# Holding DMA transposes behind the weight loads, and loading states and first x in longer rows, in a one-core attention and MLP kernel

## The chip, the cores and the metric

The kernel runs on one core of a Trainium2 chip. The metric is the device time of one execution in microseconds (us). Its profile is one profiled execution of the same program; times in it are counted from the first instruction.

Engine names: PE is the matrix engine (TensorE), DVE the vector engine, ACT the scalar engine, POOL GpSimd, SP the sync engine. POOL and SP issue transfers here as well: POOL through a software queue (it builds the descriptors itself, and can change the type on the way), SP and ACT through hardware queues.

## What is computed

For 8 batches of 8 heads, with x of 512 rows and state of 32 rows, each 64 wide, x attends to state and state attends to x; the 544 rows that come out per batch then pass through an MLP of 512 -> 2048 -> 512 with a squared ReLU, a factor s and a summand b.

```python
def _attn_ref(x, state):                      # x (8, 8, 512, 64), state (8, 8, 32, 64)
    scores = scale * np.matmul(x, state.transpose(0, 1, 3, 2))
...
    xread = np.matmul(softmax(scores), state)
    scores2 = scale * np.matmul(state, x.transpose(0, 1, 3, 2))
...
    sread = np.matmul(softmax(scores2), x)
    return np.concatenate([xread, sread], axis=2)

def _moe_ref(x, w_in, w_out, s, b):           # x (8 * 544, 512)
    r = np.maximum(x @ w_in, 0.0)
    return (s * (r * r) + b) @ w_out
```

All inputs and the output are float32; inside, the kernel works with float16 operands.

## The kernel before

**Stages of a batch.** x is laid out with 128 rows on the partitions (tile `xn`) and transposed to `xT`; for batches 0 and 1 by 16 PE matmuls with an identity (`att_xT_pe`), for batches 2 to 7 by four DMA transposes that SP issues (`att_xT_dma`, L568). States are doubled (`st16`) and transposed into `stT` (`att_st`). `part_T` makes the scores T = state x xT in 16 small matmuls, each using a part of the PE array ("tiled" mode). ACT takes their exponential E with the row sums (L663). A matmul with a block matrix of ones (`bones16`) gives the column sums D, ACT makes their reciprocal by Ln and Exp, DVE multiplies: the normalized weights `a4` (L710). `part_M` multiplies state by a quarter of the input weights (`wi`), which gives M; so x's read and the first MLP layer are one product of a4 and M (`layer1`, 8 groups of four matmuls a batch; ACT does the ReLU at L808, DVE the square at L818). The state's side: E is transposed by two DMA transposes that SP issues (`att_turn`, L730, tile `aT`), `part_V` multiplies it with xn (32 small matmuls, "V"), and the result of all batches waits until the end (`layer1_slots`). The second layer is plain for batch 0 (`layer2_first`, 64 matmuls with `wo`) and, for the others, a scheme of seven products in place of eight (`layer2`) on sums that DVE makes of the activations (`pair_sums`) and of the weights (`weight_sums`, L937).

**What orders the work.** A planner written in the kernel (`Plan`) records every operation with the engines that may do it, an estimated duration, what it reads and writes and a priority. `Plan.order` then goes through a modelled time and hands out the next operation to the engine where it can start first; the order found is issued engine by engine and never changes on the chip. Every engine runs its list in order: an instruction that waits holds all that stands behind it on that engine. A transfer has a duration `lag`: negative for loads that queue behind each other (`MB = 3.05`), positive for others. What the planner believes is only an order; on the chip an instruction waits for the data that it reads, and for the earlier users of the tile that it writes, and for nothing else. `att_turn` names `wo[3]`, the last weight load, in its `rd` list, so that the planner places the transposes behind it; but the transposes do not read `wo[3]`.

**The loads.** SP loads x of batch 0 in four pieces as float32 into `u` (L356: 128 partitions x 2 heads, rows of 256 elements = 1 KB), and ACT casts each to `xn` (L339). ACT issues the identity, the ones matrix (`bones`) and two pairs of states (`stf`). POOL issues, as software transfers with a cast, in this order: wi 0, wi 1, wo 0, x of batch 1, wi 2, wo 1, wi 3, wo 2, s, b, wo 3, the states of batches 2 to 7 (L417, tile `st`), x of batch 2. At most eight software transfers are under way: the ninth is issued when the first has landed, and so on. Later x loads are each issued behind a `gate` copy (L438) that reads the end of the previous batch's xT. POOL also issues the stores of the results (L989).

**Start.** DVE clears `warm` and PE runs 13 matmuls on it (128x512) ahead of its first real one, and a few in later gaps, chosen by the planner.

**Buffers.** PSUM is used as three pairs of banks (`ps`, in the profile "pair") and two single banks (`o`). SBUF has, among others, five `xn`, nine `g`, eight `pd`, four `u`, two `aT` and two `xT` tiles.

Of the kernel before, what the change touches and what calls it, by code (L numbers as in the profile page):

```python
# [14 lines left out]
class Op:  # L15
    def __init__(self, n, engs, fn, rd, wr, prio, mode, lag, gap):
        self.n, self.engs, self.fn, self.prio, self.mode = n, engs, fn, prio, mode
        self.lag, self.gap = lag, gap
        self.units = []
        for key in (*rd, *wr):  # L20
            if key[0] not in self.units:
                self.units.append(key[0])
        self.before = set()
        self.start = self.seen = None


class Plan:
# [10 lines left out]
    LAT = {"PE": 0.24, "ACT": 0.16, "DVE": 0.15, "POOL": 0.15}  # L38
# [23 lines left out]
    def op(self, engs, fn, rd=(), wr=(), prio=5, mode=None, lag=0.0, gap=0.0, into=(), lands=None):  # L62

        o = Op(len(self.ops), engs, fn, rd, [*wr, *((u,) for u in into)], prio, mode, lag, gap)
# [17 lines left out]
    def order(self, warm):  # L82
        free = dict.fromkeys(("PE", "ACT", "DVE", "POOL", "SP"), 0.0)
        free.update(PE=1.2, ACT=2.4, DVE=1.3, POOL=0.5, SP=0.6)
        load_free = 6.0
# [12 lines left out]
        def earliest(o, e):  # L98
            t = max(free[e], o.gap)
            for p in o.before:  # L100
                if p.eng == e and e == "PE":
                    s = p.start
                elif p.eng == e and e in ("SP", "POOL") and p.lag == 0.0:
# [21 lines left out]
        while ready:  # L125
# [39 lines left out]
            if o.lands:  # L165
                o.seen = o.lands
            elif o.lag < 0:

                begin = max(load_free, t + dur + 1.2)
                load_free = begin - o.lag  # L170
                o.seen = load_free + 0.9
            elif o.lag:
                o.seen = max(t + dur, min(load_free, t + dur + 15)) + o.lag
            else:
                o.seen = t + dur + self.LAT[e]
# [19 lines left out]
    SLACK = 0.1  # L195
# [8 lines left out]
def kernel(  # L204
# [18 lines left out]
    P = 128  # L223
# [44 lines left out]
    def PR(kind, b):  # L268
# [22 lines left out]
    st16 = sb("st16", [B * NG, 2, D])  # L291
# [12 lines left out]
    wsum = sb("wsum", [DM], FP32)  # L304
# [3 lines left out]
    bones_dr = nc.inline_tensor(  # L308
        np.kron(np.eye(4), np.ones((Ns, Ns))).astype(np.float16), name="bones_const"
    )  # L310
    st_v = state.rearrange("b (g hf) j d -> (hf j) (b g) d", g=NG)

# [3 lines left out]
    nc.vector.memset(thirty2, 1.0 / Ns)  # L316

# [7 lines left out]
    nc.scalar.dma_start(bones16, bones_dr.ap())  # L325
# [16 lines left out]
    MB = 3.05  # L342

    xf_u = [plan.unit(("u", i), "u") for i in range(2)]
    x0_v = x[0].rearrange("h (q c) d -> q h (c d)", q=P)
    xn = [plan.unit(("xn", b), "xn") for b in range(B)]

    def xf_ap(i):
        return plan.slots["u"][i // 2].bitcast(FP32).rearrange(
            "p (h f) -> p h f", h=4  # L350
        )[:, 2 * (i % 2) : 2 * (i % 2) + 2]

    def x0_load(i):
        op(
            {"SP": 0.5},
            lambda e: nc.sync.dma_start(xf_ap(i), x0_v[:, 2 * i : 2 * i + 2]),  # L356
            wr=[K(("xf", i))],
            prio=0,
            lands=(3.9, 4.7, 6.2, 6.7)[i],
        )  # L360

    def x0_cast(i):
        op(
            {"ACT": 0.55, "DVE": 0.45},
            lambda e: copy(
                e,
                T(xn[0])[:, 2 * i : 2 * i + 2].rearrange("p h c d -> p h (c d)"),
                xf_ap(i),
            ),
            rd=[K(("xf", i))],  # L370
            wr=[K(xn[0], i)],
# [3 lines left out]
    def x_load(b, h0, n, prio, rd=()):  # L375
# [9 lines left out]
            lag=-MB * n / H,  # L385
        )

    def wi_load(c, prio):
# [9 lines left out]
            lag=-MB,  # L398
        )

    def wo_load(q, prio):
# [9 lines left out]
            lag=-MB,  # L411
        )

    def st_load(prio):
        op(
            {"POOL": 1.2},
            lambda e: nc.gpsimd.dma_start(out=st16[:, 2 * NG :, 0], in_=st_v[:, 2 * NG :, :]),  # L417
            rd=[g0],
            wr=[K(("st", 2, 0))],
            prio=prio,  # L420
            lag=-1.6,
        )

    def small_load(dst, src, name, prio):
# [6 lines left out]
            lag=-0.05,  # L431
# [14 lines left out]
    for i in range(4):  # L446
# [14 lines left out]
        lambda p: st_load(p),  # L461
        lambda p: x_load(2, 0, H, p),
    ]
# [4 lines left out]
    def att_st(b0, n, tag, prio, rd=()):  # L468
        u = plan.unit(("stps", b0), tag)

        def view():
            t = T(u) if tag == "o" else T(u).rearrange("p a f -> p (a f)")
            return t.bitcast(FP16).rearrange("p (n q) -> p n q", q=P)
# [11 lines left out]
        if b0 < 2:  # L485
            op(
                {"DVE": 0.25},
                lambda e: nc.vector.tensor_copy(
                    st16[:, b0 * NG : b0 * NG + n], stf[b0].unsqueeze(2).to_broadcast((P, n, 2, D))
                ),  # L490
                wr=[key],
                prio=prio,
                gap=(4.9, 7.5)[b0],
            )
        else:
            op(
                {"DVE": 0.08 + 0.02 * n},
                lambda e: nc.vector.tensor_copy(
                    st16[:, b0 * NG : b0 * NG + n, 1], st16[:, b0 * NG : b0 * NG + n, 0]
                ),  # L500
                rd=[K(("st", 2, 0)), *rd],
                wr=[key],
                prio=prio,
            )
        op({"PE": 0.056 * n}, tr, rd=[key], wr=[K(u)], prio=prio, mode="full")
        op(
            {"DVE": 0.1 + 0.07 * n},
# [3 lines left out]
            prio=prio,  # L511
        )
# [16 lines left out]
    def att_xT_pe(b):  # L529
        u = [plan.unit(("xTps", b, i), "ps") for i in range(2)]  # L530

        def view(i):
            return T(u[i])[:, 0].bitcast(FP16).rearrange("p (h k q) -> p h k q", h=4, k=2)

        for i in range(2):

            def tr(e, i=i):
                for hh in range(4):
                    for k in range(2):
                        mm(  # L540
                            view(i)[:, hh, k, :],
                            T(xn[b])[:, 4 * i + hh, 2 * k : 2 * k + 2, :].rearrange("p c d -> p (c d)"),
                            ident16,
# [700 lines left out]
```

## Time and profile before

| | |
|---|---|
| three runs | 214.95, 215.41, 218.27 us; median 215.41 |
| profiled execution | span 211.4 us from first to last instruction; its own time outside the span is not listed |
| PE | 201.0 us busy (95%), 1966 matmuls |
| DVE, ACT, POOL | 163.8 us (77%), 111.3 us (53%), 42.1 us (20%) |
| software queue | 15360 packets, 15.40 MB |
| SP's hardware queue | 25792 packets, 8.13 MB |

The page gives busy time by engine and by line, the waits by what ended them, and the chain of work that ended last. L242 is the line of the matmul helper, so matmuls are told apart by the tiles that they write and read. A line "DMA xn<-in_x_dram" in the chain is the time from the issue of a load to its landing.

### The profile page before, as it was taken

What the parts mean: (1) busy time and instruction counts of PE and PEld (TensorE: products, weight loads), DVE (VectorE), ACT (ScalarE), POOL (GpSimd) and SP (SyncE); (2) the same over time, 40 slices, a digit from 0 to 9 for tenths busy, and PEclk for the clock granted to TensorE, in tenths of its full rate; (3) what the DMA queues carried; (4) which work ended last, traced back from release to release, by engine and by line L of the source; (5) the groups of instructions that cost most, each with busy time, mean ns of one, the idle gap of its engine ahead of it and who ended that gap; (6) DMA issues with size and microseconds to landing.
All of it is one profiled execution on the core that took longest, in us unless ns stands there. A gap on an engine that the chain in (4) does not pass through costs nothing.

```text
span 211.4 us, 4751 instructions
## 1 busy us (share of the span) xinstructions
PE 201.0 (95%) x1966; PEld 132.3 (63%) x1966; DVE 163.8 (77%) x309; ACT 111.3 (53%) x154; POOL 42.1 (20%) x64
## 2 busy tenths in 40 slices
PE   7985699999999999999999999999999999999992
PEld 2432343445746764767575755776588588888882
DVE  0664779999579989997995989976996697675452
ACT  3594599700778779563877588714910780040000
POOL 5820300042131140303411141114111111111000
PEclk9999999999999999999999999999999999999999
DMA  6999999558798596496596741222011210112132
GB/s 188 220 190 157 207 198 168 93 157 112 166 138 119 102 119 205 76 158 134 72 202 127 82 131 53 50 65 99 12 51 56 85 50 30 57 68 97 55 124 74
DMA packets 42007, 24.04 MB, mean 114 GB/s; under 512 B 26369, under 2 KB 40193, under 8 KB 41985
## 3 DMA queue, kind: packets, MB, share of 16 engines
q0 software_dynamic: 15360, 15.40, 39.6%
q1 hardware_dynamic: 25792, 8.13, 21.0%
q8 instruction: 15, 0.25, 0.5%
q10 hardware_dynamic: 832, 0.20, 0.4%
q14 instruction: 8, 0.06, 0.1%
HBM read 17.37 MB, written 8.91 MB: 124 GB/s over the span
## 4 chain that ended last, share of the span: by engine, by line
PE 81%; DMA 8%; DVE 5%; ACT 2%; POOL 1%; issue 1%
PE o L242 47%; PE pair L242 34%; DMA xn<-in_x_dram 7%; ACT E L663 2%; DVE g L818 1%; DVE u L937 1%; DMA ident<-ident_const 1%; POOL wi L391 1%; DVE xT L339 1%; DVE M L339 1%; POOL wo L404 0%; DVE osb L1026 0%; DVE bias_bc L980 0%; ACT a L703 0%; DVE wsp L966 0%
## 5 line engine op out<-in xcount | busy, mean ns | idle before, releaser
L808 ACT ACTIVATE g<-pair 128x1024 f16<-128x1024 f32 x64 | 61.2, 1035 | 26.6 <-PE pair L242 26.6
L242 PE MATMUL pair<-a,M 128*128 128x512 f16 x256 | 59.6, 379 | 0.2
L242 PEld LDWEIGHTS <-g 128*128 128x128 f16 x424 | 40.9, 98 | 18.3 <-issue 3.0
L242 PEld LDWEIGHTS <-pd 128*128 128x128 f16 x480 | 46.3, 98 | 8.9 <-issue 2.5
L818 DVE TENSOR_TENSOR g<-g 128x1024 f16<-128x1024 f16 x64 | 43.1, 685 | 9.0 <-ACT g L808 9.0
L242 PE MATMUL o<-wo,g 128*128 128x256 f16 (+1 forms) x304 | 44.9, 295 | 0.2 <-DVE osb L1026 0.2
L242 PE MATMUL o<-u,pd 128*128 128x256 f16 x360 | 42.5, 273 | 0.0
L242 PEld LDWEIGHTS <-M 128*128 128x128 f16 x256 | 25.0, 98 | 26.4 <-issue 0.4
L989 POOL DMA_DIRECT2D out_dram<-osb x28 | 18.7, 671 | 95.3 <-DVE osb L1097 38.0
L1085 DVE SCALAR_TENSOR_TENSOR osb<-o,s_bc,bias_bc 128x512 f32<-128x512 f32 (+1 forms) x32 | 22.8, 714 | 10.5 <-PE o L242 10.1
L1097 DVE SCALAR_TENSOR_TENSOR osb<-o,s_bc,osb 128x512 f32<-128x512 f32 (+1 forms) x24 | 17.2, 715 | 8.9 <-PE o L242 8.7
L663 ACT ACTIVATE E<-pair 128x512 f16<-128x512 f32 x16 | 9.4, 593 | 25.9 <-PE pair L242 25.9
L899 DVE TENSOR_TENSOR pd<-g 128x1024 f16<-128x1024 f16 (+1 forms) x32 | 20.7, 653 | 0.2
L339 DVE CAST M<-pair 128x1024 f16<-128x1024 f32 x16 | 19.5, 1218 | 1.7 <-PE pair L242 1.6
L339 ACT CAST M<-pair 128x1024 f16<-128x1024 f32 x16 | 16.1, 1014 | 7.9 <-PE pair L242 7.9
L242 PE MATMUL o<-u,g 128*128 128x256 f16 x120 | 16.7, 273 | 0.0
L242 PE MATMUL o<-wo,pd 128*128 128x256 f16 x120 | 14.6, 273 | 0.0
L907 DVE TENSOR_TENSOR pd<-g,pd 128x512 f16<-128x512 f16 (+1 forms) x32 | 12.6, 403 | 0.2
L910 DVE TENSOR_TENSOR pd<-g,pd 128x512 f16<-128x512 f16 (+1 forms) x32 | 12.6, 403 | 0.2
L858 ACT ACTIVATE g<-pair 128x256 f16<-128x256 f32 x16 | 5.3, 381 | 12.7 <-PE pair L242 12.7
L766 POOL COPY srd<-srdT 128x128 f16<-128x128 f16 x8 | 7.6, 950 | 19.6 <-DMA srdT<-sr 19.6
L242 PE MATMUL pair<-wi,stT 64*32 64x512 f16 x256 | 10.3, 382 | 0.5 <-DMA wi<-in_moe_w_in_dram 0.5
(52 smaller groups left out, 125.0 us busy)
## 6 DMA issues: line engine op xcount, KB each, us to landing
out_dram<-osb POOLq DMA_DIRECT2D x28, 256.0 KB, 2.7
xn<-in_x_dram POOLq DMA_DIRECT2D x7, 512.0 KB, 6.8
wi<-in_moe_w_in_dram POOLq DMA_DIRECT2D x4, 512.0 KB, 12.8
wo<-in_moe_w_out_dram POOLq DMA_DIRECT2D x4, 512.0 KB, 19.1
u<-in_x_dram SPq DMA_DIRECT2D x4, 256.0 KB, 4.3
out_dram<-osb SPq DMA_DIRECT2D x4, 256.0 KB, 2.5
out_dram<-osb SPq DMA_DIRECT2D x4, 128.0 KB, 2.3
xT<-xn SPq DMA_TRANSPOSE x24, 2.5
```

Source lines behind the costliest of these rows:

```text
L242: return nc.tensor.matmul(out, lhsT, rhs, start=start, stop=stop, tile_position=tp, is_transpose=is_transpose, skip_group_check=True,)
L339: (nc.scalar.copy if e == "ACT" else nc.vector.tensor_copy)(dst, src)
L663: nc.scalar.activation(T(E[b])[:, g, :].rearrange("p (m t) -> p m t", m=2), T(u)[:, :, hS * g : hS * g + hS], AF.Exp, scale=scale, accum_o ...
L766: lambda e: nc.gpsimd.tensor_copy(srd[:, :, :, b], srdT[:, b]),
L808: lambda e, u=u, j=j, p=p: nc.scalar.activation(g_view(G[b, j])[:, 2 * p : 2 * p + 2], T(u), AF.Relu),
L818: nc.vector.tensor_mul(t, t, t)
L899: nc.vector.tensor_tensor(view()[:, :, 0:2], blocks(b, j)[:, :, 1:2, :].to_broadcast((P, 2, 2, n)), blocks(b, j)[:, :, 0:4:3, :], ALU.subt ...
L907: nc.vector.tensor_tensor(view()[:, :, 2], blocks(b, j)[:, :, 3], view()[:, :, 0], ALU.subtract)
L910: nc.vector.tensor_tensor(view()[:, :, 3], blocks(b, j)[:, :, 2], view()[:, :, 2], ALU.subtract)
L989: lambda e: eng(e).dma_start(dst, src()),
L1085: lambda e: nc.vector.scalar_tensor_tensor(t_view(u), o_view(bank), s_bc, bias(h), ALU.mult, ALU.add),
L1097: lambda e: nc.vector.scalar_tensor_tensor(t_view(u), o_view(bank), s_bc, t_view(u), ALU.mult, ALU.add),
```

## The change

1. **Transposes of E for batches 0 and 1.** `att_turn(b, True)` now has POOL copy two elements of `wo[3]` into each half of `aT` (the new helper `after`). The transpose writes the same tile, so it waits for the copy, and the copy waits for the last weights.
2. **States of batches 2 to 7.** The software load with cast, the DVE copy that doubles them, the 12 PE transposes (128x128) and the DVE copy go. In their place: after a like copy of two elements, SP loads 96 rows of 1024 float32 (4 KB) into a `pd` buffer; two POOL copies (96x1024, float32 to float16) double them into another `pd` buffer; 16 PE transposes (96 columns) go into one PSUM pair; ACT or DVE copies the pair to `stT`.
3. **x of batch 0.** Pieces are cut so that a partition holds eight rows (512 elements, 2 KB) of one head; `part_T` and the exponential of batch 0 read and write in the matching order. The cast tile `xe` serves the scores only. For `part_V`, x of batch 0 is loaded a second time by POOL, as the last of the first loads.
4. **The ones matrix** is made by five DVE memsets, not loaded.
5. **The planner.** In place of `lag`, transfers are on a software or a hardware queue with a service time each; a ninth transfer of a kind waits for the first of eight; several estimated durations are changed. The order of nearly everything changes with it.

In the built program the POOL list becomes: ..., wo 3, x 2, x 0, five two-element copies, the two state copies, the gate for x 3, x 3, ... and the SP list: four x pieces, the states, two transposes of E 0, four of x 2, two of E 1, ... (before: two of E 0, two of E 1, four of x 2, ...). The number of warm matmuls goes from 13 and 7 to 13 and 5.

```diff
-    LAT = {"PE": 0.24, "ACT": 0.16, "DVE": 0.15, "POOL": 0.15}
+    LAT = {"PE": 0.24, "ACT": 0.16, "DVE": 0.13, "POOL": 0.25, "SP": 0.1}
...
+            if o.dma and len(landed[o.dma[0]]) >= 8:
+                t = max(t, landed[o.dma[0]][-8])
...
+            if o.dma:
+                kind, service = o.dma
+                begin = t + dur + self.REACH[kind]
+                if kind == "sw":
+                    begin = max(begin, dma_free["sw"])
+                    done = begin + service
+                    dma_free["sw"] = done
+                else:
+                    begin = max(begin, dma_free["hw"])
+                    busy = dma_free["sw"] > begin
+                    done = begin + service * (2 if busy else 1)
...
+    REACH = {"sw": 1.2, "hw": 0.5}
+    RECEIPT = {"sw": 1.0, "hw": 0.6}
...
+    PS = (B - 2) * H * 2
+    st_rows = state[2:].rearrange("b h (v r) d -> (b h v) (r d)", v=2)
...
+    nc.vector.memset(bones16, 0.0)
+    for q in range(4):
+        nc.vector.memset(bones16[Ns * q : Ns * q + Ns, Ns * q : Ns * q + Ns], 1.0)
...
-    nc.scalar.dma_start(bones16, bones_dr.ap())
...
-    MB = 3.05
+    MB, XB = 2.5, 3.3
...
-    x0_v = x[0].rearrange("h (q c) d -> q h (c d)", q=P)
+    x0_v = x[0].rearrange("(i h) (q c) d -> (h q) i (c d)", i=4, c=8)
...
-            lambda e: nc.sync.dma_start(xf_ap(i), x0_v[:, 2 * i : 2 * i + 2]),
+            lambda e: nc.sync.dma_start(xf_ap(i), x0_v[:, i]),
...
+    def after(tile, key, src, rd):
+
+        op(
+            {"POOL": 0.2},
+            lambda e: nc.gpsimd.tensor_copy(tile(), src()),
+            rd=rd,
+            wr=[key],
+            prio=0.5,
+        )
...
+    def st_load():
+        after(
+            lambda: flat(stf2)[:, 0:2],
+            K(stf2),
+            lambda: wo[3][:, 3, DM - 2 : DM],
+            [K(("wo", 3))],
+        )
+        op(
+            {"SP": 0.5},
+            lambda e: nc.sync.dma_start(flat(stf2).bitcast(FP32)[0:PS], st_rows),
...
-        lambda p: st_load(p),
         lambda p: x_load(2, 0, H, p),
+        lambda p: x_load(0, 0, H, p),
...
+    def att_st_rest():
...
+        for k in range(2):
+            op(
+                {"POOL": 1.3},
+                lambda e, k=k: nc.gpsimd.tensor_copy(wide()[:, :, k], rows()),
...
+        op({"PE": 0.8}, tr, rd=[K(stw, 0), K(stw, 1)], wr=[K(u)], prio=6, mode="full")
+        op(
+            {"ACT": 1.4, "DVE": 1.7},
+            lambda e: copy(
...
-                dur += 0.43
+                dur += 0.32
...
-    def att_turn(b, rd=()):
+    def att_turn(b, late=False):
+        if late:
+            after(
+                lambda: T(aT[b])[:, 0, 0, 0:2],
+                K(aT[b], 0),
+                lambda: wo[3][:, 3, DM - 2 : DM],
+                [K(("wo", 3))],
+            )
...
-    att_turn(0, [K(("wo", 3))])
+    st_load()
+    att_turn(0, True)
...
-    att_st(2, (B - 2) * NG, "ps", 6, [K(a4[1], 1)])
+    att_st_rest()
```

## Prediction, made before the change had run

> **What bounds the kernel now.** I read the page first, its busy table and its slices: PE is the bound, and all that PE loses lies in the first 26 us and the tail.
>
> ```profile
> PE 201.0 (95%) x1966; PEld 132.3 (63%) x1966; DVE 163.8 (77%) x309; ACT 111.3 (53%) x154; POOL 42.1 (20%) x64
> PE   7985699999999999999999999999999999999992
> ```
>
> A slice is 5.3 us; from the sixth on PE is full to the last. So the change can win only what PE loses early, and can lose anywhere. Next, PE's waits (total, times, longest) and the chain of work that ended last (start, length, what):
>
> ```profile
> PE pair L242 <- DMA xn<-in_x_dram: 2.2, 1, 2.2
> PE pair L242 <- ACT E L663: 1.2, 3, 0.8
> PE pair L242 <- ACT a L703: 0.7, 1, 0.7
> PE pair L242 <- DMA wi<-in_moe_w_in_dram: 0.5, 2, 0.3
> ```
>
> ```profile
> 5.07 15.67 DMA xn<-in_x_dram
> 20.79 0.64 PE pair L242 x8
> ```
>
> The load of x for batch 1, issued at 5.07, lands at 20.8: the largest wait of PE, and the chain hangs on it. Then the busy times in stretches of 2 us (PE, PEld, DVE, ACT, POOL, clock, DMA share, GB/s) and the order of time:
>
> ```profile
> 16.00:18.00 2.00, 2.00 (x11) 0.93 (x10) 1.40 (x3) 2.00 (x3) 0.06 (x1) 1.00 1.39 193
> 18.00:20.00 2.00, 0.55 (x3) 0.05 (x1) 0.69 (x1) 0.04 (x1) 0.00 (x0) 1.00 1.41 97
> 22.00:24.00 2.00, 1.00 (x24) 0.34 (x16) 1.86 (x3) 0.73 (x3) 0.86 (x2) 1.00 1.23 205
> 24.00:26.00 2.00, 1.28 (x19) 0.49 (x19) 1.36 (x3) 1.97 (x5) 0.07 (x1) 1.00 1.25 207
> ```
>
> ```profile
> 1.19 5.49 PE L242 MATMUL o<-warm 128*128 128x512 f16 x13 [1.19 <-DVE warm L314]
> 10.32 16.17 SPq L730 DMA_TRANSPOSE aT<-E  x4
> 20.79 1.07 PE L242 MATMUL pair<-ident,xn 128*128 128x128 f16 x16 [2.24 <-DMA xn<-in_x_dram]
> ```
>
> Loads alone move 200 to 207 GB/s; in 18 to 20 us, with transposes of E under way, 97. Those transposes go out at 10.32, though the planner put them behind wo 3. Last, the issues of single loads (KB, us to landing):
>
> ```profile
> wi<-in_moe_w_in_dram POOLq DMA_DIRECT2D x1, 512.0 KB, 7.0
> wo<-in_moe_w_out_dram POOLq DMA_DIRECT2D x1, 512.0 KB, 10.7
> xn<-in_x_dram POOLq DMA_DIRECT2D x1, 512.0 KB, 15.7
> st<-in_state_dram POOLq DMA_DIRECT2D x1, 192.0 KB, 15.6
> xn<-in_x_dram POOLq DMA_DIRECT2D x1, 512.0 KB, 15.5
> ```
>
> Issue plus time gives the landings before: wi 0 9.7, wi 1 12.1, wo 0 15.0, x 1 20.8, wi 2 22.95, wo 1 25.5, wi 3 27.9, wo 2 31.5, wo 3 34.7, states 36.6, x 2 38.7. Undisturbed steps are 2.15 to 2.55; wo 0 and x 1 together took 8.7, wo 2 and wo 3 6.8.
>
> **The change part by part.**
>
> *Transposes held.* wo 2 and wo 3 beside two transposes took 6.8 in place of 2 x 2.45: a pair costs the loads 1.9. x 1 alone takes between 2.1 (states to x 2) and 8.7 - 2.45 - 1.9 = 4.35. Counted in the packet records, an x load undisturbed at 65 us moves 390 of its 1024 packets per us, so I take 2.65. Then wo 0 lands at 14.6, x 1 at 17.3 (16.7 to 19.0), wi 2 19.8, wo 1 22.3, wi 3 24.8, wo 2 27.3, wo 3 29.8: up to 5 us earlier. What is late next is in the sum.
>
> *x of batch 0 in 2 KB rows.* Half the packets, so the pieces land earlier, by 0 to 1.5 us (the first software packet goes out at 5.9, the last x piece lands at 7.15). But PE stands behind its 13 warm matmuls until 6.5 either way, and the second half of xT moves from a DVE copy (0.69) to an ACT copy (1.03). First MLP matmul before: 12.96, held by wi 1 (12.1) and the chain through ACT. I take 12.9; ends 12.4 and 13.3. If the software loads start earlier as well, by 0 to 1.2 us, that is a rival below.
>
> *Ones matrix.* One load of 32 KB goes, for which nobody waited; five memsets (0.09 to 0.27 each) lie in the 4.1 us that DVE idles until 5.4. Without that cover: 0.7 us.
>
> *States.* The DVE copies (0.35 and 0.96) and a POOL issue (1.03) go, all beside a full PE. 12 PE transposes took 0.67; 16 at the same price take 0.90: +0.23 on PE. ACT's copy of 1536 columns: 1.03 x 1.5 = 1.5.
>
> *Order, and the sum.* With the measured durations (group of four MLP matmuls 0.865, second-layer matmul 0.216, 16 tiled matmuls 0.65, a pair of D 0.43, V 0.42) the new PE list runs: four groups from 12.9, one second-layer matmul: 16.8. x 1 at 17.3, transposes 1.07: 18.4. Seven second-layer: 19.9. wi 2 is there (19.8): 20.55. T waits for ACT's copy of M: 21.5, then 0.4: 21.9. Groups, D and eight second-layer matmuls, 3.9: 25.8. **wo 2 comes at 27.3: 1.5 of waiting stay.** Then 1.05, three groups, the bias sums 1.05 (wo 3 is there), two groups and 0.8: 34.5. Five groups: 38.85. State transposes: 39.75. V of batch 0: 40.2. Before, V ended at 40.82 + 0.42 = 41.24 with the state transposes (0.67) still to do: 41.9. Gain so far 1.7.
>
> *What the new order asks for at 39 to 43 us.* After V come eight second-layer matmuls (1.73) and 16 tiled ones: T of batch 2 stands at 42.6, where before it stood at 53.3. It needs the four transposes of x 2, behind the states and two transposes of E 0 on SP's queue. Work in the transfers from 29.8: x 2 2.65, x 0 2.65, states 1.0 (393 KB read; a weight load reads 1 MB in 2.45), six transposes of 1.2 each (SP's row, x4 in 5.1): 13.5, so 43.3 and 0.5 to land. T can use the first ones earlier; I take 0.5 to 1.0 us of waiting, ends 0 and 2.5. So the gain is 1.7 - 0.2 (ACT's copy of the states, ready about then) - 0.7 = 0.8, and 0.3 more since PE waited 0.4 in all after 45 us before (ACT E, osb) and T now runs earlier there: 1.1.
>
> *Behind the new waits.* On POOL, behind the five small copies (0.19 to 0.43) and the state copies, stand the gate and load of x 3 and the stores; x 3 is issued at about 44 (before: 46.1) and lands 6.8 later as before, at 51; its transposes take 6.6 more, and T of batch 3 stands by the new list about 14 us behind T of batch 2, at 57. No wait is priced here, but the slack is small. On SP, behind the states' load, stand the transposes of E 0, wanted at 39.7. The end of the program is the same list as before: 0.
>
> *POOL's state copies.* 1024 elements a partition, twice. The nearest rows are POOL's copies of 128 elements, 0.76 to 1.23, and of 2 elements, 0.19. Scaled per element: (0.76 - 0.19) / 126 x 1024 = 4.6 each; the other end is DVE's cast of 256 elements, 0.45, x 4 = 1.8, or less. The row of 128 writes single elements 16 bytes apart, the new copy runs of 64, so I stand near the low end: 1.8 each. With the states landed at 34.3, they are done at 37.9, PE asks at 38.85. The Trainium skill, GPSIMD Engine Reference, section 3.1, puts a one-input loop at about 1.8 cycles an element at best: by estimate 1.5 us a copy, and no wait of PE. Scaled from the row it would be 43.5 and a wait of 4.7; no run here yet shows which. The same page, section 8, says that POOL shares its SBUF interfaces with DVE, which speaks against putting the copies on POOL. The trace shows that small: a DVE sum of 512 took 0.54 beside a POOL copy at 103.07, and 0.41 alone.
>
> **The rivals.**
>
> A. *The wait moves to 39 to 43 us.* For: 13.5 us of transfers in 13 us, and transposes beside loads took 7.4 to 9.8 to land, not 2.5. Against: T takes its pieces one by one. Price 1.5 to 3.0 beyond the forecast: 215.1 to 217.2, taken 216.0. It decides from x 2's last transpose landing after 44.
>
> B. *POOL's copies hold PE* (the slower side): at 4.6 us each the state transposes start at 43.5 in place of 38.85: 214.3 + 4.7 = 219.0. It decides from 2.3 us a copy on. For: the row of 128. Against: the cast on DVE.
>
> C. *Loads also start earlier.* If x 0's longer rows let the software stream start 1.2 us earlier, wo 2 comes at 26.1, the wait for it falls from 1.5 to 0.3, and x 2 lands sooner: another 1.2 to 2, so 212.5.
>
> D. *The change does not do what it says*: x 1 is no earlier, because it is slow by itself (4.35). Then x 1 lands at 19.0 and all loads behind it come 1.7 later, wo 2 too, so that nothing is made up there: 1.1 - 1.7 = -0.6, 216.0. For: x 1 and wo 0 together took 8.7. Against: the 390 packets per us at 65 us.
>
> **How the numbers follow.** The span was 211.4; the median of the runs is 215.41, 4.0 more, and the change leaves what lies around the span alone. 215.4 - 1.1 = 214.3. Its own range is 213.1 to 215.1: chance 0.45. A 0.24, B 0.07, C 0.18 (211.0 to 213.1), D 0.06. The range leaves out B and the far end of C: 211.7 to 217.2, about 0.85. Two per cent of 215.4 is 4.3 us, about what a measurement of this kernel can tell from no change (one of three runs stood 1.3% above the other two): faster would be below 211.1, only the far end of C, 0.05; slower above 219.7, the far end of B, 0.04; the rest 0.91.
>
> **What would show it.** Right: no transpose of E before wo 3's landing; x 1 landing near 17.3; PE's wait for xn near 0.5; a wait for wo of about 1.5 near 26; T of batch 2 near 43 with under 1 us of waiting. Wrong: POOL's state copies over 2.3 us each; a PE wait for transposes of xT or for xn over 1.5; loads that still fall to 100 GB/s without transposes beside them; DVE late with osb at 45 us, because POOL's copies held it.

## The result, and the profile after

The changed kernel takes 218.5 us in the median of 20 runs, the kernel before 216.47 in 20 runs. Executions come in a faster and a slower state, and ratios here and below compare those in the faster one alone (12 of the 20 for the changed kernel), so they need not be the ratio of the medians: 1.0134, 95% interval 1.0089 to 1.0179. It is slower by 1.3%, where 214.3 and a gain of 1.1 us were forecast. The profiled execution has a span of 215.8 (before: 211.4).

PE's waits after (total, times, longest), to be held against those of before:

```profile
PE pair L254 <- POOL pd L554: 2.0, 1, 2.0
PE o L254 <- DMA wo<-in_moe_w_out_dram: 1.6, 1, 1.6
PE pair L254 <- DMA wi<-in_moe_w_in_dram: 1.2, 3, 0.5
PE pair L254 <- DMA wo<-in_moe_w_out_dram: 0.7, 1, 0.7
PE pair L254 <- DMA xn<-in_x_dram: 0.5, 1, 0.5
```

The wait for x 1 (`xn`) fell from 2.2 to 0.5, as the change means it to. In its place stand two waits for the last weights and one for the state copies. PE's timeline puts them in order (start, duration, what, and in brackets the wait ahead of it):

```profile
17.91 1.07 PE L254 MATMUL pair<-ident,xn 128*128 128x128 f16 x16 [0.50 <-DMA xn<-in_x_dram]
...
28.57 0.38 PE L254 MATMUL o<-wo,g 128*128 128x512 f16 x1 [1.57 <-DMA wo<-in_moe_w_out_dram]
...
33.85 0.40 PE L254 MATMUL pair<-wo,ones 128*32 128x512 f16 x4 [0.67 <-DMA wo<-in_moe_w_out_dram]
...
43.05 0.85 PE L254 MATMUL pair<-ident,pd 96*128 96x96 f16 x16 [2.00 <-POOL pd L554]
43.83 0.42 PE L254 MATMUL pair<-xn,aT 128*32 128x64 f16 x32
44.18 3.45 PE L254 MATMUL o<-wo,g 128*128 128x512 f16 x8
```

Up to 17.9 PE is ahead of the kernel before (20.8 for the same transposes). Then it runs into wo 2, wo 3 and the states. The last line is the price of the clock: eight matmuls of 128x512 take 3.45, or 0.43 each in place of 0.216, because 1.3 us after the wait the granted clock drops to half, from 44.4 to 47.8 (its mean is 0.59 in 44 to 46 and 0.56 in 46 to 48; the 44.6 and 48.0 in an expectation below are read 0.2 too late). The chain of work that ended last says what was late behind what (start, length, what):

```profile
15.49 18.32 DMA wo<-in_moe_w_out_dram
33.86 0.80 POOL pd L436
34.69 5.50 DMA pd<-in_state_dram
40.32 2.68 POOL pd L554 x2
```

wo 3 was issued at 15.49 and lands at 33.8; then POOL's small copy takes 0.8, the states' load 5.5, then POOL's two copies 2.7, and only then come the state transposes, ahead of V and T in PE's list. The stretches (busy time of PE, PEld, DVE, ACT, POOL, then clock, DMA share, GB/s) show when wo 3 was lost:

```profile
24.00:26.00 2.00, 2.00 (x11) 0.89 (x10) 0.89 (x3) 1.92 (x4) 0.00 (x0) 1.00 1.25 207
26.00:28.00 2.00, 1.00 (x5) 0.37 (x4) 0.84 (x2) 2.00 (x5) 0.00 (x0) 1.00 0.95 156
28.00:30.00 2.00, 1.43 (x20) 0.45 (x20) 1.13 (x3) 0.94 (x2) 0.00 (x0) 1.00 0.80 128
30.00:32.00 2.00, 2.00 (x11) 0.88 (x9) 2.00 (x5) 1.65 (x3) 0.00 (x0) 1.00 1.27 190
```

From 26 to 30 the transfers fall from 207 to 128 GB/s, and no transpose is under way. In the packet records only two things stand at that place of the software queue: the loads of s and b, ahead of wo 3. Each is 32 packet records there, 16 of 32 bytes and 16 of 4 (14848 packets in the queue, 14784 when experiment 1 takes the two loads out), not the 128 small packets that an expectation below speaks of; issued through ACT's hardware queue in experiment 1, each is 144 packets of 4 bytes (688 in that queue, then 976). They were there in the kernel before too, where wo 2 and wo 3 ran beside transposes. Their rows, first of the changed kernel, issued at 10.24 and 12.76, then of the kernel before, issued at 10.01 and 12.47 (KB, us to landing):

```profile
s_bc<-in_moe_s_dram POOLq DMA_DIRECT2D x1, 0.5 KB, 20.7
b_bc<-in_moe_b_dram POOLq DMA_DIRECT2D x1, 0.5 KB, 18.5
...
s_bc<-in_moe_s_dram POOLq DMA_DIRECT2D x1, 0.5 KB, 21.6
b_bc<-in_moe_b_dram POOLq DMA_DIRECT2D x1, 0.5 KB, 19.3
```

In the changed kernel wo 2 lands at 28.5, s at 31.0, b at 31.25, wo 3 at 33.8: from wo 2 to b it takes 2.7, and wo 3 then its own 2.55. In the kernel before, b lands at 31.8, only 0.4 behind wo 2 (31.4).

How much of the difference is clock? Each run lists its span and its mean granted clock; span times one minus the clock is what half clock cost it at most. The kernel before lost 2.0 on average in the runs beside the first experiments (9 runs, span 213.2), the changed kernel 2.3 (12 runs, span 215.8). So nearly all of the difference, 2.3 us (213.5 against 211.2 without those losses), is other than clock. The profiled execution of before happened to run at full clock.

### The profile page after: what moved, and what is told of

It reads as the page before. It is cut to its first block, busy times and chain, and to the rows that moved or that the text cites. A ratio compares the mean times of both kernels' runs of the same rounds, so it can differ in the third digit from the quotient of the medians.

```text
span 215.8 us, 4764 instructions
## 1 busy us (share of the span) xinstructions
PE 202.9 (94%) x1968; PEld 132.5 (61%) x1968; DVE 165.4 (77%) x312; ACT 113.8 (53%) x155; POOL 46.7 (22%) x71
## 3 DMA queue, kind: packets, MB, share of 16 engines
q0 software_dynamic: 14848, 15.73, 38.9%
## 4 chain that ended last, share of the span: by engine, by line
PE 76%; DMA 17%; POOL 2%; ACT 2%; issue 1%; DVE 0%; POOLq 0%
PE o L254 47%; PE pair L254 30%; DMA wo<-in_moe_w_out_dram 13%; DMA pd<-in_state_dram 3%; ACT E L747 2%; POOL pd L554 1%; DMA ident<-ident_const 1%; POOL wi L406 1%; POOL pd L436 0%; DVE osb L1182 0%; POOL gate L474 0%; POOL aT L436 0%; POOLq L554 0%
## 5 line engine op out<-in xcount | busy, mean ns | idle before, releaser
L905 ACT ACTIVATE g<-pair 128x1024 f16<-128x1024 f32 x64 | 61.9, 1024 | 38.7 <-PE pair L254 38.5
L254 PEld LDWEIGHTS <-pd 128*128 128x128 f16 (+1 forms) x496 | 47.2, 98 | 9.9 <-POOL pd L554 2.5
L915 DVE TENSOR_TENSOR g<-g 128x1024 f16<-128x1024 f16 x64 | 43.9, 697 | 10.7 <-ACT g L905 10.5
L254 PE MATMUL o<-wo,g 128*128 128x256 f16 (+1 forms) x304 | 47.5, 301 | 1.6 <-DMA wo<-in_moe_w_out_dram 1.6
L254 PE MATMUL o<-u,pd 128*128 128x256 f16 x360 | 41.8, 273 | 0.0
L351 DVE CAST M<-pair 128x1024 f16<-128x1024 f32 x17 | 20.6, 1216 | 4.8 <-PE pair L254 4.8
L996 DVE TENSOR_TENSOR pd<-g 128x1024 f16<-128x1024 f16 (+1 forms) x32 | 20.8, 652 | 0.2
L351 ACT CAST M<-pair 128x1024 f16<-128x1024 f32 x15 | 15.2, 1013 | 10.9 <-PE pair L254 10.9
L863 POOL COPY srd<-srdT 128x128 f16<-128x128 f16 x8 | 9.7, 1208 | 23.9 <-DMA srdT<-sr 23.9
## 6 DMA issues: line engine op xcount, KB each, us to landing
wi<-in_moe_w_in_dram POOLq DMA_DIRECT2D x4, 512.0 KB, 11.6
wo<-in_moe_w_out_dram POOLq DMA_DIRECT2D x4, 512.0 KB, 17.3
```

The costliest lines, as they stand in the source:

```text
L254: return nc.tensor.matmul(out, lhsT, rhs, start=start, stop=stop, tile_position=tp, is_transpose=is_transpose, skip_group_check=True,)
L351: (nc.scalar.copy if e == "ACT" else nc.vector.tensor_copy)(dst, src)
L863: lambda e: nc.gpsimd.tensor_copy(srd[:, :, :, b], srdT[:, b]),
L905: lambda e, u=u, j=j, p=p: nc.scalar.activation(g_view(G[b, j])[:, 2 * p : 2 * p + 2], T(u), AF.Relu),
L915: nc.vector.tensor_mul(t, t, t)
L996: nc.vector.tensor_tensor(view()[:, :, 0:2], blocks(b, j)[:, :, 1:2, :].to_broadcast((P, 2, 2, n)), blocks(b, j)[:, :, 0:4:3, :], ALU.subt ...
```

## The experiments

The theory after reading the traces: the hold works, but the two broadcast loads of s and b stall the stream that it freed, and what the new order hangs on wo 3 (states, POOL's copies, V and T) comes too late. The rivals: the hold costs by itself; the loss is one of clock; the states are too late whatever the weights do.

**1. s and b by ACT, at the start** (changed kernel).

```
     nc.scalar.dma_start(stf[1], ...)
+    nc.scalar.dma_start(s_bc, moe_s.to_broadcast((P, 1)))
+    nc.scalar.dma_start(b_bc, moe_b.to_broadcast((P, 1)))
...
-        lambda p: small_load(s_bc, moe_s, "s", p),
-        lambda p: small_load(b_bc, moe_b, "b", p),
```

> The changed kernel with the two 4-byte broadcast loads (s, b) issued by ACT at the start in place of POOL, ahead of wo 3; every engine's list is otherwise the same. Theory 1 (the two tiny loads stall some of the transfer engines ahead of wo 3, and the chain wo 3, states, POOL copies then holds PE): wo 3 lands near 31.0 in place of 33.8, the states near 37.4, PE waits for POOL at the state transposes 0 to 0.6 us in place of 2.0, the clock stays full from 41 to 50, span near 212, ratio to the kernel before 0.985 to 1.0. Rival (wo 3 is late because x 2 and x 0 share the queue behind it): wo 3 still lands after 33, PE still waits about 2.0, ratio near 1.013.

Measured: 1.0298 (1.0228 to 1.0368), against the forecast. The stall of 26 to 30 is gone, but a stall now lies at the start. Stretches of this run:

```profile
6.00:8.00 2.00, 1.41 (x17) 0.96 (x15) 1.09 (x3) 0.40 (x1) 2.00 (x3) 1.00 0.33 64
...
26.00:28.00 2.00, 2.00 (x11) 0.93 (x10) 0.86 (x2) 1.92 (x4) 0.00 (x0) 1.00 1.24 206
28.00:30.00 2.00, 0.92 (x5) 0.29 (x3) 0.92 (x2) 2.00 (x5) 0.00 (x0) 1.00 1.24 206
```

In 6 to 8 us, where the changed kernel moves 180 GB/s, it is 64. The last piece of x 0 came late, and PE waited 3.3 for its cast (ACT's row: 3.58 idle for the DMA). So the two loads cost 2 to 3 us of everybody's transfers in this queue too. POOL's rows, first of the changed kernel, then of this run, show the stream of loads from the issue that wi 0's landing released to the copy of the end of wo 3:

```profile
10.24 0.56 POOL L463 DMA_DIRECT2D s_bc<-in_moe_s_dram  x1 [0.91 <-DMA wi<-in_moe_w_in_dram]
...
33.86 0.80 POOL L436 COPY pd<-wo 128x2 f16<-128x2 f16 x1 [11.77 <-DMA wo<-in_moe_w_out_dram]
```

```profile
12.73 0.74 POOL L421 DMA_DIRECT2D wo<-in_moe_w_out_dram  x1 [2.95 <-DMA wi<-in_moe_w_in_dram]
...
32.94 0.43 POOL L438 COPY pd<-wo 128x2 f16<-128x2 f16 x1 [14.20 <-DMA wo<-in_moe_w_out_dram]
...
40.39 5.17 POOL L554 CAST pd<-pd 96x1024 f16<-96x1024 f32 x2 [5.41 <-DMA pd<-in_state_dram]
```

The stream takes 32.94 - 12.73 = 20.2, in the changed kernel 33.86 - 10.24 = 23.6. Without s and b it is 3.4 shorter; 2.7 of that is the stretch between wo 2 and b, the rest came ahead of wo 2, and its cause was not looked for.

The start is not the whole loss. What was expected at the states did not come either. They land at 40.25, as before, although wo 3 is 0.9 earlier, and the last row shows POOL's two copies at 5.17, not 2.67: the first alone takes 4.19, beside DVE products that keep their 0.41 and 0.68 up to 43.7. PE waits 3.57 for the copies, and half clock follows (46.7 to 50.1).

**2. Warm matmuls in the new wait** (changed kernel).

```
         def tr(e):
+            for _ in range(10):
+                mm(T(u)[:, 0], warm[:, 0:P], warm)
             for r in range(16):
```

> The changed kernel with ten warm matmuls (128x512, 2.2 us) on the same PSUM pair ahead of the state transposes, nothing else moved. Theory 1 (the wait of 2.0 us lets the matmul clock fall to half from 44.6 to 48.0, which costs 1.7 us more): the clock stays full in 40 to 50, the wait for POOL shrinks to about 0.2 (it is filled, not saved), eight second-layer matmuls behind V take 1.9 in place of 3.45, span near 214.1, ratio near 1.005. Rival (the slow matmuls have another cause, such as a busy port or PSUM): they stay near 3.4 and the span near 215.8, ratio near 1.013.

Measured: 1.0152 (1.0087 to 1.0216), against the forecast of 1.005. The clock did as expected: the eight matmuls behind V take 1.90, and the runs lose 0.8 to it in place of 2.3. But their spans without that loss are 215.1 on average in place of 213.5. The ten matmuls buy clock and cost about as much; why they cost 1.6, where the profile shows the wait filled and only 0.75 of new waits near 73, stays open. The clock alone is not the loss.

**3. The hold alone** (kernel before, with four POOL copies that tie `aT` to wo 3).

```
         if rd:
+            for g in range(NG):
+                after(lambda g=g: T(aT[b])[:, g, 0, 0:2], K(aT[b], g),
+                      lambda: wo[3][:, 3, DM - 2 : DM], [K(("wo", 3))])
```

> The kernel before with the hold alone: four two-element POOL copies of wo 3 into aT, so that the transposes of E 0 and E 1 wait for wo 3. Theory 1: x 1 lands near 17.9 (before 20.8) and PE's wait for it falls from 2.2 to about 1.0 or less; wo 3 does not gain (33.5 to 34.5), the transposes of E 0 go out near 34.5 and land near 41, and V of batch 0, which PE reaches near 39, waits about 2: span 210.5 to 212, ratio 0.99 to 1.005. Rival (the hold is a clean gain of 2 to 3 us, and the rest of the change loses it): no wait at V, span near 209, ratio near 0.987.

Measured: 1.0132 (1.0061 to 1.0204). This is above both expectations: one part of the change, holding the transposes, loses as much as the whole. From the issue that wi 0 released to wo 3 it takes 24.2 here; s and b land 3.6 behind wo 2. PE does not wait for x 1, and 0.7 for wo 3. But the wait of 2 at V of batch 0 did not come (V begins at 40.2), and the waits that the profile shows lie later: 2.4 in all for transposes of x at 75 to 78, and 1.5 for one of E at 127.9. So the run shows that the hold loses, but not yet by which path.

**4. s and b by ACT in the kernel before**, the same edit as in 1.

> The kernel before with s and b loaded by ACT at the start, nothing else moved. Theory 1: wo 2 to wo 3 takes 2.5 to 3.0 in place of 3.25 and wo 3 lands 0.5 to 1.5 earlier than 34.7, although the transposes of E run beside it; PE does not wait for wo 3 in this kernel, so the time stays: ratio 0.995 to 1.005. Rival (only the transposes slow those loads): wo 3 stays at 34.7, ratio 1.0.

Measured: 1.002 (0.9977 to 1.0064), the time as expected. The loads were not earlier: the start loses time (134 GB/s in 6 to 8, before 207), and wo 3 lands at 37.7, three microseconds later than before. From wo 2 to wo 3 it takes 2.7, as expected, but wi 3 to wo 3 together 6.4, only 0.4 less than before. In the profile PE waits 6.3 for x and the first weights; where it makes that up was not looked into.

**5. s and b as one element each** (changed kernel). POOL, idle then, loads them at 1.3 us into one partition; a 128x2 matmul beside the bias sums and a DVE copy spread them.

```
+    nc.gpsimd.memset(bias_bc[0:1, 0:P], 1.0)
+    nc.gpsimd.dma_start(out=sb_in[0:1, 0:1], in_=moe_s.to_broadcast((1, 1)))
+    nc.gpsimd.dma_start(out=sb_in[0:1, 1:2], in_=moe_b.to_broadcast((1, 1)))
...
+            mm(T(v)[:, 1, 0:2], bias_bc[0:1, 0:P], sb_in[0:1, :])
```

> The changed kernel, but s and b are loaded as one element each by POOL at the very start and spread over the partitions by one 128x2 matmul and a DVE copy, in place of two broadcast loads of 128 small packets in the middle of the software stream. Theory (those two loads stall the stream for 3.4 us and make wo 3, and with it the states, late): wo 3 lands near 30 in place of 33.8, the states near 35, PE waits less than 0.5 for the state copies in place of 2.0, and the ratio to the kernel before is 0.983 to 1.000. Rival (the hold costs by itself, because everything behind wo 3 comes too late anyway): the ratio stays 1.008 to 1.018.

Measured: 1.0045 (1.0005 to 1.0084): about two thirds of the loss are gone, the rest stays, between the two expectations. wo 3 lands at 32.25 and the states at 38.7, later than the 30 and 35 that were expected. Its timeline, POOL and PE:

```profile
11.93 0.75 POOL L423 DMA_DIRECT2D wo<-in_moe_w_out_dram  x1 [2.23 <-DMA wi<-in_moe_w_in_dram]
...
32.30 0.33 POOL L440 COPY pd<-wo 128x2 f16<-128x2 f16 x1 [14.32 <-DMA wo<-in_moe_w_out_dram]
```

```profile
29.69 0.38 PE L254 MATMUL o<-wo,g 128*128 128x512 f16 x1 [1.54 <-DMA wo<-in_moe_w_out_dram]
...
41.56 0.84 PE L254 MATMUL pair<-ident,pd 96*128 96x96 f16 x16
...
49.15 2.53 PE L254 MATMUL o<-wo,g 128*128 128x512 f16 x11 [1.34 <-DVE osb L1129]
```

From wi 0 to wo 3 it is 32.30 - 11.93 = 20.4, as in 1, although wi 0 released POOL 1.7 later than in the profile of the changed kernel (11.93 against 10.24). PE does not wait for the states, and the runs lose 1.1 to the clock, not 2.3. That is most of the gain: without the clock losses the spans are 213.2 on average, against 213.5 for the changed kernel. What is left are waits of 3.1 for the late wi 0 and wi 1, the wait for wo 2, which was forecast, and a new one of 1.34 for DVE's `osb`.

**6. No hold at all** (changed kernel without the five POOL copies).

```
-            lambda e: nc.gpsimd.tensor_copy(tile(), src()),
+            lambda e: None,
```

> The changed kernel without the five two-element POOL copies, so that the states and the transposes of E 0 and E 1 wait for nothing but their own data; all other lists are the same. Theory (the chain behind wo 3 is what was lost): x 1 is late again (near 20.5, PE waits about 2 for it), the states land before 15, PE waits for no state copy at 41, and the ratio is 0.998 to 1.010. Rival (the hold is a gain, and the loss comes from another part of the change): slower than the changed kernel, 1.018 or more.

Measured: 1.0157 (1.0094 to 1.0219), between the two expectations. x 1 is late again (PE waits 1.7 for it, at 21.4) and the states wait for nothing. But SP issues them at 2.6, PE waits 1.7 for the cast of the last piece of x 0, and the first weights come later: the issue that wi 0's landing releases is at 12.08, not 10.24. That the states' bytes are paid there is likely, not shown: the kernel of 11, which loads no states then, has 12.11.

**7. s and b as one element each in the kernel before.**

> The kernel before with s and b loaded as one element each, as above. Theory (in the kernel before PE is so far behind at 31 to 35 us that it never waits for wo 2 or wo 3): the loads land up to 3 us earlier, the time moves by less than 0.5 per cent, ratio 0.994 to 1.003. Rival (the stall costs in any order of work): 0.985 or less.

Measured: 1.0028 (0.9984 to 1.0071), the time as the theory has it. But its reason does not hold: the loads do not land up to 3 us earlier. From wi 3 (28.2) to wo 3 (35.1) it takes 6.9, before 6.8. So beside the transposes the same two loads cost 0.4 us at most, which is how far b landed behind wo 2 in the kernel before.

**8. The hold ends with x 1** (changed kernel; the POOL copies read the end of x 1).

```
-                lambda: wo[3][:, 3, DM - 2 : DM],
+                lambda: T(xn[1])[:, H - 1, SCH - 1, D - 2 : D],
```

> The changed kernel with the same five POOL copies, but reading the end of x 1 and not of wo 3, so the states and the transposes of E are let go at about 22. Theory (what comes beside the weights costs their time, 1.9 for the states and 1.9 for a pair of transposes): x 1 still lands near 18, wo 2 lands 3 to 4 us later than 28.6 and PE waits for it 4 to 5 in place of 1.6, no wait for the state copies; ratio 1.010 to 1.025. Rival (only the late states cost; the weights have slack): 0.995 to 1.003.

Measured: 1.0214 (1.0162 to 1.0265), as the theory has it; the runs lose 4.0 to the clock, so that the time is not the late weights alone. States and transposes beside the weights make wo 2 late:

```profile
32.83 0.58 PE L254 MATMUL o<-wo,g 128*128 128x512 f16 x1 [5.47 <-DMA wo<-in_moe_w_out_dram]
```

5.5 of waiting in place of 1.6. The weights have no slack in the new order.

**9. The hold alone, with s and b as one element each** (3 and 7 together, no other change).

> The kernel before with the transposes of E 0 and E 1 held behind wo 3 by four POOL copies (as in the run with the hold alone) and with s and b loaded as one element each. Theory (the hold by itself lost 1.3 per cent because it lays the stall of the two broadcast loads bare): the ratio to the kernel before falls to 0.995 to 1.006. Rival (what the hold loses is the late transposes themselves, whatever the weights do): 1.010 to 1.020.

Measured: 0.9912 (0.9872 to 0.9952). This is faster than the kernel before (medians of all runs 213.71 against 214.87 us), and better than the theory asked for. Its POOL and PE:

```profile
11.35 0.74 POOL L408 DMA_DIRECT2D wo<-in_moe_w_out_dram  x1 [1.89 <-DMA wi<-in_moe_w_in_dram]
...
31.60 1.90 POOL L732 COPY aT<-wo 128x2 f16<-128x2 f16 x4 [14.25 <-DMA wo<-in_moe_w_out_dram]
```

```profile
PE pair L242 <- DMA wi<-in_moe_w_in_dram: 2.6, 2, 2.0
...
PE pair L242 <- DMA xT<-xn: 1.0, 1, 1.0
PE pair L242 <- ACT E L665: 0.8, 1, 0.8
PE pair L242 <- ACT a L705: 0.7, 1, 0.7
PE pair L242 <- DMA aT<-E: 0.6, 1, 0.6
```

20.25 from wi 0 to wo 3, and neither x 1 nor wo 2 nor wo 3 among the waits. The same hold is worth -1.2% without the broadcast loads (0.9912 against 1.0028) and cost +1.3% with them. The clock does not make this: without its losses the spans are 1.5 below the kernel before here, and 2.3 above it in 3. So the hold by itself is no loss; together with the two loads it is.

**10. Warm matmuls in the old wait** (kernel before, nine of them ahead of the transposes of x 1, as in 2).

> The kernel before with nine warm matmuls ahead of the transposes of x 1, in PE's wait of 2.2 at 18.5 to 20.8. Theory (runs of the kernel before lose 2 to 3 to half clock, and most of it follows from this wait, as after the long waits in four of the traces): the mean clock of its runs rises from about 0.99 to 0.996 or more, ratio 0.988 to 0.996. Rival (the half clock follows from later waits, as for xT at 75): clock and time as before, 0.998 to 1.004.

Measured: 1.0125 (1.0073 to 1.0176), against both expectations. The runs lose 2.3 to the clock, no less than before. In the profile the half clock lies at 11.9 to 15.3, after a wait of 2.3 for wi 0:

```profile
11.27 0.41 PE L242 MATMUL pair<-wi,stT 64*32 64x512 f16 x8 [2.28 <-DMA wi<-in_moe_w_in_dram]
```

So the losses of the kernel before do not hang on x 1 alone. In this profile PE also came to the nine matmuls only at 20.2, since wi 0 was late, while x 1 landed at 20.6: they ran to 22.2, filled 0.4 of waiting and cost about 1.6. Whether the other runs lost it in the same way is not known.

**11. More POOL copies** (kernel of 5; four copies of 96x512 that nobody needs behind the two state copies).

```
+                    [nc.gpsimd.tensor_copy(warm[0:PS], flat(stf2).bitcast(FP32)[0:PS, 0:512]) for _ in range(4 * k)],
```

> The changed kernel with s and b as one element each, and behind POOL's two state copies four more POOL copies of 96x512 into the warm tile, which nobody needs: POOL's work of about 41 to 44 is doubled, and PE's list does not wait for it. Theory (POOL's copies slow DVE beside them: there two DVE products took 1.26 and 1.52 in place of 0.42 and 0.68, and PE then waited 1.3 for DVE's osb): DVE loses another 1.2 to 2, PE waits 2.3 to 3.5 for osb, ratio 1.008 to 1.016. Rival (DVE is late for another reason): no change, 1.000 to 1.006.

Measured: 1.0101 (1.0064 to 1.0138), against 1.0045 without them. DVE's row, the useful copies at 39.15 to 41.5 and the added ones to 45.0:

```profile
39.37 1.26 DVE L1039 TENSOR_TENSOR u<-wo 128x512 f16<-128x512 f16 x1
40.55 1.52 DVE L920 TENSOR_TENSOR g<-g 128x1024 f16<-128x1024 f16 x1
41.99 0.82 DVE L1039 TENSOR_TENSOR u<-wo,u 128x512 f16<-128x512 f16 x1
42.74 1.09 DVE L920 TENSOR_TENSOR g<-g 128x1024 f16<-128x1024 f16 x1
...
45.52 0.41 DVE L1039 TENSOR_TENSOR u<-wo,u 128x512 f16<-128x512 f16 x1
45.85 0.68 DVE L920 TENSOR_TENSOR g<-g 128x1024 f16<-128x1024 f16 x1
```

The same products take 0.41 and 0.68 when POOL is idle: beside each long copy one of them loses 0.84, beside each short one 0.41. The four added copies cost DVE 1.64, and PE waits 1.88 for V's result (`sr`), ahead of the wait for `osb`, which stays 1.34: 3.2 together, as expected, though not at the place expected. The two state copies cost DVE 1.68 in the same way. That the two state copies are also behind the 1.34 of kernel 5 is likely from this, not shown: a run without them was not made.

Whom the contention holds is not fixed. Here POOL keeps to 1.2 a copy and DVE is slowed; in 1, DVE kept its times and POOL's first copy took 4.19.

**12. wo 2 ahead of wi 3** (kernel of 5; the two loads change places, nothing else).

> The changed kernel with s and b as one element each, and the loads of wi 3 and wo 2 issued in the other order; nothing else differs. Theory (of what is left over the kernel before, 1.5 is PE's wait for wo 2, which the new order of work asks for before it can be there): wo 2 lands 2.5 earlier, PE does not wait for it, waits up to 0.7 for wi 3 instead, and the ratio falls from 1.0045 to 0.997 to 1.002. Rival (the wait only moves on, to wi 3 or to DVE): 1.003 to 1.008.

Measured: 0.9995 (0.9958 to 1.0031). PE's waits:

```profile
PE pair L254 <- DMA wi<-in_moe_w_in_dram: 2.3, 3, 1.4
...
PE o L254 <- DVE osb L1135: 1.1, 1, 1.1
```

The wait for wo 2 is gone, one of 1.4 for wi 3 (at 28.3) stands in its place, twice what was expected, and DVE is still late with `osb`. The runs lose 0.6 to the clock, and the kernel before lost 2.4 beside them (1.8 beside 5). Without these losses the spans are 1.6 above the kernel before, in 5 they were 1.9 above it. So most of the fall of 0.5% is clock, and the intervals of the two runs overlap: the new order of the two loads is not shown to gain.

## Why the prediction was wrong

**x 1: right.** Forecast 17.3 for its landing and 0.5 for PE's wait; measured 17.9 and 0.50. That the wait fits so well is partly luck: PE was 0.6 late as well (its first MLP matmul began at 13.34, not 12.9). The cause was right: x 1 was slow for the transposes, not by itself. Its own step was 2.66 (2.65 was forecast, 4.35 by rival D), so D is refuted.

**wo 3: the step that failed.** "wo 2 27.3, wo 3 29.8" put an undisturbed step between the two; the loads of s and b, which stand there in the queue, got no price and no word. It rested on the reading that wo 2 and wo 3 took 6.8 before only because of two transposes ("a pair costs the loads 1.9"). That reading was right for the kernel before (7: without the broadcast loads they took 6.9). But s and b cost next to nothing only beside the transposes (0.4 at most). Without transposes they took 2.7 in the changed kernel and 3.6 in 3, and the whole stream is 3.4 to 4.0 longer with them (1, 5, 9 against the changed kernel and 3). wo 3 landed at 33.8, 4.0 late: 2.7 by s and b, and 1.25 because wo 2 was late already. The prediction priced the stall that goes and did not ask what it had covered.

**wo 2** landed at 28.5, 1.25 late, and s and b stand behind it. Of this, 0.6 is there at wo 0 (15.2, forecast 14.6) and another 0.6 comes from wi 2, which took 3.1 behind x 1 in place of 2.5. Why is open.

**The states.** 34.3 was forecast, 40.2 measured: 4.0 of that from wo 3, and 1.9 because from wo 3 to the states it took 6.4, not 4.5. "States 1.0" counted their bytes; the load took 5.5 behind the packets of x 2 and x 0, and landed with x 0 (40.2 and 40.3), as it did in 1 and 5. In 5, with wo 3 at 32.25, POOL's copies were done at 41.2 and PE, which came at 41.56, did not wait.

**The sum.** V of batch 0 was to end at 40.2 and ended at 44.25. Of the 4.05, 1.27 is wo 2, 0.67 the wait for wo 3, 2.0 the states. The 0.7 of waiting for T of batch 2 did not come, since PE was late itself. 4.05 - 0.7 = 3.35 turns a gain of 1.1 into a loss of 2.25; the runs without clock losses gave 2.3. This takes all that lies behind V as unchanged, which was not checked, and 5 warns of it: there the wait for the states is gone, and most of it is back in other waits. So the sum says where the lead was lost up to 44 us, not that taking the stall away gives it back.

**POOL's copies.** 1.8 each was taken, 1.33 measured; so rival B (4.6 each) was not what made this kernel slow. But one run shows a copy nearly that long (4.19 in 1, and 3.57 of waiting), and not for the reason that B gave: a copy alone takes 1.03 (8), under the least that the prediction estimated (1.5). And "the trace shows that small" for DVE beside POOL was wrong: DVE lost 1.7 beside the two copies, and once the states were in time PE waited for `osb`, a sign that the prediction had named. The Trainium skill, SBUF — State Buffer, section "Who interferes with whom", says that a DVE instruction with two SBUF inputs contends with a GpSimd instruction that reads SBUF. The trace agrees: 0.41 became 1.26, and all slowed products have two such inputs. The row that the prediction used instead showed 0.13 beside a copy of 128 elements. By the 0.84 beside a copy of 1024 one would expect 0.1: it was the same price, for a copy an eighth as long.

**Rivals.** A was right in the place (39 to 43 us), but too small (216.0, at most 217.2, against 218.5), and not in its cause: what PE waited for was the states. The last transpose of x 2 did land at 44.9, after the 44 that A named, but PE came for it only at 48.1. C did not show: wi 0 landed at 10.0 in the profile, before at 9.7.

**The clock.** The sum took the 4.0 between the profiled span and the median as fixed. Half of it is half clock, which the profiled run did not have and most runs do. It did not move the ratio here, since both kernels lose about as much (2.0 and 2.3).

**The rest of the change.** With s and b out of the way the hold alone gives 0.9912, the whole change 1.0045. What it has beyond the hold thus costs 1.3%: an order of work that reaches wo 2 before it is there (waits of about 1.5; 12 moves the wait and does not show a gain), and probably POOL's copies, which make DVE late. How the loss is shared among these, the states, the longer rows, the second load of x 0 and the new order stays open.

## What to carry to other kernels

When a change takes away a stall, list everything else that stands in the same queue at that time: a cost that the old stall covered can come back in full (here 0.4 at most became 2.7 to 3.6). Price a transfer by its place in the queue and a measurement there, not by its bytes: two loads of 4 bytes to 128 partitions took more than a weight load of half a megabyte (2.5), and one element with a matmul to spread it cost nothing that could be measured (7: 1.0028, interval 0.9984 to 1.0071). And before work is hung on the last transfer, follow the whole chain (load, copies, who runs beside the copies) up to PE's list.

## What was not expected of the hardware

- Two broadcast loads of 4 bytes to 128 partitions stalled a queue that had 207 GB/s: 2.7 and 3.6 us in the software queue, and in ACT's hardware queue at the start the transfers fell to 64 GB/s in 6 to 8 us. Beside DMA transposes they cost 0.4 at most. The mechanism was not looked into.
- Half clock came after PE's waits of 2 to 5.5 us, within 2 us of their end or before it: after 2.00 that ended at 43.05 (from 44.4), after 3.25 and 3.57 in experiment 1 (ends 10.7 and 45.6, half clock from 12.6 and 46.7), after 2.28 in 10 (end 11.3, from 11.9), after 2.47 in 4 (end 23.0, from 24.7), after 1.97 in 9 (end 11.1, from 12.2), during 2.50 in 11 and 5.47 in 8 (from 11.6 and 30.6). In 3, 6 and 7 it came after or between shorter waits (0.8 to 1.7). It did not come after 2.24 in the profile before, nor after 2.16 in 5, nor after 2.37 in 7. It lasted 3.41 us or twice that each time, but for the last microseconds of the program. The Trainium skill, TensorE: Matmul & The Clock Gate, section "What's actually happening", tells of free-running windows of 3413 ns and of a drop after at least one idle window; the lengths agree, but waits shorter than a window were enough here.
- wi 0, the first load of the software queue, led to POOL's next issue at 9.8 to 11.0 us in kernels that are the same up to there (2: 9.81; changed: 10.24; 8: 11.01), and the kernel before with its two variants spreads as far (10.01; 3: 11.20; 10: 11.51). Such a shift moves all that follows, and single profiles should be compared from that landing on.
